# Loads moved: batch 2's k and v from batch 0's FFN to the start of batch 1's, and later loads a step or two back

## The chip, the cores and the metric

The kernel runs on one core of a Trainium2 chip. Its time is the device time of one execution in microseconds (us). An engine of the core takes its instructions strictly in the order of its own queue; the engines are TensorE (PE, with weight loads shown as PEld), VectorE (DVE), ScalarE (ACT), GpSimd (POOL) and SyncE (SP, which here issues nearly all DMAs). An instruction waits at the head of its queue until the semaphores it needs have arrived.

## The reference, cut to what matters

Attention with a packed query p (32 rows per head) in two softmax steps, then an FFN with softplus, for 8 batches of 576 tokens, 8 heads of 64, and a hidden width of 2048:

```python
p_packed = sm_attn(p, k, v)                # 32 packed rows per head
out = sm_attn(q, p_packed, p_packed)
x = out.transpose(0, 2, 1, 3).reshape(B * S, H * D)
h = x @ w_in
g = np.maximum(h, 0.0) + np.log1p(np.exp(-np.abs(h)))
return g @ w_out
```

The activations are float32. The weights are float64 and are converted on the chip.

## The kernel before, in words

**Stages.** Attention of batch 0 runs first, alone but for the conversion of the first weights. Then a loop runs over 128 units, 16 to a batch (variable `u`; unit u is batch u // 16, and f = u % 16 is a block of 128 hidden columns). A unit does `gemm1` (12 matmuls of line 585), the softplus of its two halves, and `gemm2_tile` for the unit two before it (12 matmuls of line 623). Every unit has four slots (the loop over t). In each slot a counter `due` grows by PACE = 0.56, and each time it passes 1 the attention of the next batch goes one step further: `attention_first` for batches 0 and 1, `attention_next` from batch 2 on (FIRST = 2). A step ends at a `yield`. So the attention of batch 1 runs inside the FFN of batch 0 (units 0 to 15), and that of batch 2 inside the FFN of batch 1 (units 16 to 31). What of it is left in the last unit of a batch is run to its end there, and `weights` then makes the operands of the next batch's gemm1.

**Weights.** In batch 0's FFN a second counter does the same with `convert`, 1.6 steps a slot. It goes through 32 blocks, named i0 to i15 for w_in and o0 to o15 for w_out, in the order i0 i1 o0 o1 i2 i3 o2 o3 and so on. A block is loaded into an x slot (`load64`, line 150, two DMAs for w_in, one for w_out); there are two such slots, so a block can only be loaded when the block two before it has been read. Then ACT makes m and r of it (lines 192, 196), DVE t (198, 203), POOL the sum (211), and for w_out ACT and DVE make the two halves (230, 236). `make_m` (line 548) reads the converted w_in: it runs on PE every second unit in batch 0, and the call at the end of unit 10 needs i12 and i13, the one at the end of unit 12 needs i14 and i15.

**Loads.** q, k and v have one pool of four buffers, `ld`. Each tile is half a batch (four heads). A load takes the buffer of the tile that was used up last: batch 2's two k tiles take those of batch 1's v, which are free after `packed` (line 310), and batch 2's two v tiles those of batch 1's q. From batch 2 on, k and q come as four DMAs of 144 KB each (line 137) and are turned by DVE in place (`quads`, line 246), and v as one DMA of 576 KB (line 129). Before the change, k of the next batch is loaded in the step that runs `packed`, v in the step before `scores2` (batch 1's attention) or with it (later), and q right behind the two `scores1` that read k. `load_pack` loads p for two batches with two DMAs (line 99), in the last unit of every second batch.

**Order.** PE's order is that of the text of the program: the kernel is built under `manual_schedule` for PE alone. For the other queues, DVE, ACT, POOL and SP with its DMAs, a planner lays down a fixed order when the kernel is built: it plays the program through with its own estimates of time, gives every engine what is ready, and among ready instructions the one that stands first in the text. On the chip that order does not change any more.

Where batch 2's loads stand in the text before: k half 0 in unit 5, k half 1 in unit 8, v half 0 in unit 9, v half 1 in unit 12. Among them stand the loads of the blocks o10 to o15 and i12 to i15.

Of the kernel before, what the change touches and what calls it, by code (L numbers as in the profile page):

```python
# [26 lines left out]
def pack_attention_then_softplus_ffn(  # L27
# [19 lines left out]
    G = H * J // P  # L47
# [7 lines left out]
    FIRST = 2  # L55
# [186 lines left out]
    def quads(nm, b, g):  # L242
        t = loaded[nm, b, g]
        for o in range(0, HG, 2):
            x = t[:, o:o + 2, :].rearrange("x h n -> x (h n)")
            nc.vector.transpose(x, x)
        return [t[:, hh, :] for hh in range(HG)]
# [113 lines left out]
    def attention_first(b):  # L361


        a1 = [work.tile([P, S], F32, tag="a1", name=f"a1_{b}_{g}") for g in range(G)]
        pp = [None] * G
        kT, qT = [], []
        for hh in range(HG):
            kT.append(transposed("k", b, 0, hh))
            yield
        load("q", b, 0)  # L370
        for c in range(2):
            scores1(b, 0, c, kT, a1[0])
        yield
        nm = softmax1_max(b, 0, a1[0])
        kT = [transposed("k", b, 1, 0)]
        yield
        z0 = softmax1_exp(b, 0, a1[0], nm)
        kT.append(transposed("k", b, 1, 1))
        yield
        rs0 = softmax1_sum(b, 0, z0)  # L380
        for hh in range(2, HG):
            kT.append(transposed("k", b, 1, hh))
            yield
        load("q", b, 1)
        for c in range(2):
            scores1(b, 1, c, kT, a1[1])
        yield
        nm = softmax1_max(b, 1, a1[1])
        a1T = work.tile([NP, SI, P], F32, tag="a1T", name=f"a1T_{b}_0", bufs=1)
        for c in range(2):  # L390
            a1_transposed(b, 0, c, a1[0], a1T)
            yield
            if c == 0:
                z1 = softmax1_exp(b, 1, a1[1], nm)
        rs1 = softmax1_sum(b, 1, z1)
        pp[0] = packed(b, 0, a1T, rs0)
        load("k", b + 1, 0)
        yield
        qT.append(transposed("q", b, 0, 0))
        yield  # L400
        a1T = work.tile([NP, SI, P], F32, tag="a1T", name=f"a1T_{b}_1", bufs=1)
        for c in range(2):
            a1_transposed(b, 1, c, a1[1], a1T)
            yield
        res[b]["pt"].append(packed_transposed(b, 0, pp[0]))
        yield
        qT.append(transposed("q", b, 0, 1))
        yield
        pp[1] = packed(b, 1, a1T, rs1)
        load("k", b + 1, 1)  # L410
        yield
        for hh in range(2, HG):
            qT.append(transposed("q", b, 0, hh))
            yield
        load("v", b + 1, 0)
        a2 = scores2(b, 0, 0, qT)
        a2n = scores2(b, 0, 1, qT)
        yield
        softmax2_exp(b, 0, 0, a2)
        res[b]["pt"].append(packed_transposed(b, 1, pp[1]))  # L420
        yield
        qT = [transposed("q", b, 1, 0)]
        softmax2_div(b, 0, 0, a2)
        a2 = a2n
        yield
        qT.append(transposed("q", b, 1, 1))
        softmax2_exp(b, 0, 1, a2)
        yield
        qT.append(transposed("q", b, 1, 2))
        yield  # L430
        qT.append(transposed("q", b, 1, 3))
        softmax2_div(b, 0, 1, a2)
        yield
        load("v", b + 1, 1)
        a2 = scores2(b, 1, 0, qT)
        a2n = scores2(b, 1, 1, qT)
        yield
        softmax2_exp(b, 1, 0, a2)
        yield
        softmax2_exp(b, 1, 1, a2n)  # L440
        softmax2_div(b, 1, 0, a2)
        yield
        softmax2_div(b, 1, 1, a2n)
        yield

    def attention_next(b):


        a1 = [work.tile([P, S], F32, tag="a1", name=f"a1_{b}_{g}") for g in range(G)]
        kT = [quads("k", b, 0)]  # L450
        yield
        yield
        for c in range(2):
            scores1(b, 0, c, kT[0], a1[0])
        load("q", b, 0)
        yield
        nm = softmax1_max(b, 0, a1[0])
        kT.append(quads("k", b, 1))
        yield
        z0 = softmax1_exp(b, 0, a1[0], nm)  # L460
        yield
        for c in range(2):
            scores1(b, 1, c, kT[1], a1[1])
        load("q", b, 1)
        yield
        rs0 = softmax1_sum(b, 0, z0)
        nm = softmax1_max(b, 1, a1[1])
        yield
        a1T = work.tile([NP, SI, P], F32, tag="a1T", name=f"a1T_{b}_0", bufs=1)
        for c in range(2):  # L470
            a1_transposed(b, 0, c, a1[0], a1T)
            yield
            if c == 0:
                z1 = softmax1_exp(b, 1, a1[1], nm)
        yield
        rs1 = softmax1_sum(b, 1, z1)
        pp = [packed(b, 0, a1T, rs0)]
        load("k", b + 1, 0)
        qT = [quads("q", b, 0)]
        yield  # L480
        a1T = work.tile([NP, SI, P], F32, tag="a1T", name=f"a1T_{b}_1", bufs=1)
        for c in range(2):
            a1_transposed(b, 1, c, a1[1], a1T)
            yield
        res[b]["pt"].append(packed_transposed(b, 0, pp[0]))
        yield
        pp.append(packed(b, 1, a1T, rs1))
        load("k", b + 1, 1)
        qT.append(quads("q", b, 1))
        yield  # L490
        a2 = scores2(b, 0, 0, qT[0])
        a2n = scores2(b, 0, 1, qT[0])
        load("v", b + 1, 0)
        yield
        res[b]["pt"].append(packed_transposed(b, 1, pp[1]))
        yield
        softmax2_exp(b, 0, 0, a2)
        yield
        softmax2_div(b, 0, 0, a2)
        yield  # L500
        softmax2_exp(b, 0, 1, a2n)
        yield
        softmax2_div(b, 0, 1, a2n)
        yield
        a2 = scores2(b, 1, 0, qT[1])
        a2n = scores2(b, 1, 1, qT[1])
        load("v", b + 1, 1)
        yield
        softmax2_exp(b, 1, 0, a2)
        yield  # L510
        softmax2_div(b, 1, 0, a2)
        yield
        softmax2_exp(b, 1, 1, a2n)
        yield
        softmax2_div(b, 1, 1, a2n)
        yield
# [154 lines left out]
    for f in range(NF):  # L671
        if f % 2 == 0:
            order += [("i", f), ("i", f + 1)]
        order.append(("o", f))
    PACE = 0.56
    CONV = 1.6
    CONV_EARLY = 1.6
    CONV_STEP = 14
# [14 lines left out]
    due = 0.0  # L693
# [12 lines left out]
    ahead, chain, due = iter(()), iter(()), 0.0  # L706
    for u in range(len(units) + LAG):
        if u < len(units):
            b, f = units[u]
            if f == 0:  # L710
                if (b + 1) % BG == 0 and b + 1 < B:
                    pack_transposed((b + 1) // BG, pt)
                ahead = attention(b + 1) if b + 1 < B else iter(())
                due = 0.0
            chain = softplus(b, f, gemm1(b, f, res[b]), gs)
            next(chain)
            if f == NF - 1:
                if (b + 2) % BG == 0 and b + 2 < B:
                    pt = load_pack((b + 2) // BG, (nc.sync,))
                for _ in ahead:  # L720
                    pass
                if b + 1 < B:
                    weights(b + 1)
        if u >= LAG:
            b2, f2 = units[u - LAG]
            gh, gl = gs.pop((b2, f2))
            if f2 == 0:
                acc = [ps_acc.tile([P, DM], F32, tag="acc", name=f"acc_{b2}_{t}") for t in range(NT)]
        last = u >= LAG and f2 == NF - 1 and b2 % 2 == 1
        if last:  # L730
            both = rests(b2)
            next(both)
        for t in range(NT):
            if u >= LAG:
                gemm2_tile(
                    acc[t], gh, gl, f2, slice(t * P, (t + 1) * P), f2 == 0, f2 == NF - 1
                )
                if f2 == NF - 1:
                    store(acc[t], [(0, b2, t * P, P)], f"{b2}_{t}")
            if u < len(units):  # L740
                due += PACE
                while due >= 1:
                    next(ahead, None)
                    due -= 1
                if b == 0:
                    cdue += CONV
                    while cdue >= 1:
                        next(conv, None)
                        cdue -= 1
            next(chain, None)  # L750
        if last:
            next(both)
        if u + 2 < len(units):


            nb, c = units[u + 2][0], units[u + 2][1] * P
            if c % m_cols(nb) == 0:
                make_m(nb, c // m_cols(nb), res[nb])
# [29 lines left out]
```

## Time and profile before

| | |
|---|---|
| time, median of 3 runs | 816.55 us (815.74 to 820.81) |
| profiled execution | 816.35 us, span 814.6 us, mean granted clock 0.963 |
| PE busy | 743.3 us, 91% |
| DVE busy | 540.4 us, 66% |
| ACT busy | 440.6 us, 54% |
| POOL busy | 93.8 us, 12% |
| HBM read, written | 45.61 MB, 9.44 MB |

The page divides the span into 40 slices and gives each engine's busy share in tenths; 9 means 90% or more. The other views used below are: sums over stretches of the span; the waits, which give for each instruction that waited the one that released it, with the total in us, the count and the longest; and the timeline, with start and duration in us, engine, line of the kernel, operation and tiles, and in square brackets the idle time before it with its releaser. A tile is written by its name in the program: m, r and t are the steps of the conversion, x_i and x_o are raw weight blocks, psm is make_m's product, ps that of the scores, T_q a transposed q, a the attention scores.

The starts of units given below are those of the first matmul of line 585 of a unit.

### The profile page before, as it was taken

How to read it: one execution, taken by the hardware profiler on the slowest of the kernel's cores; microseconds unless marked ns; L12 is line 12 of the kernel's file. 1: busy time of each engine (PE TensorE's matmuls, PEld its weight loads, DVE VectorE, ACT ScalarE, POOL GpSimd, SP SyncE). 2: the span in 40 equal slices, each digit the busy share in tenths (PEclk: the TensorE clock that was granted, in tenths of full speed). 3: DMA queues.
4: the chain of work that ended last, by engine and by line, in shares of the span. 5: the costliest groups of instructions: out<-in, count | busy, mean ns of one | idle time of the engine just before them, and what ended most of it. 6: DMA issues, size and time to landing. Idle time of an engine off the chain costs nothing.

```text
span 814.6 us, 14337 instructions
## 1 busy us (share of the span) xinstructions
PE 743.3 (91%) x5360; PEld 585.6 (72%) x5360; DVE 540.4 (66%) x1220; ACT 440.6 (54%) x1089; POOL 93.8 (12%) x166
## 2 busy tenths in 40 slices
PE   5478994499999989999999999999999899999997
PEld 3256674277788767886788777877788687887886
DVE  3688866856696647856686647766786647665544
ACT  6558854566555345565555345565556254565550
POOL 1414321310000000000000000100000000001010
PEclk9968996699999989999999999999999999999999
DMA  9976834505410334105410333105410310010002
GB/s 230 237 164 158 191 88 101 133 14 111 89 30 1 82 52 79 30 8 111 89 30 2 83 64 64 31 17 103 80 30 1 89 35 2 1 39 14 1 1 65
DMA packets 149669, 55.97 MB, mean 69 GB/s; under 512 B 116320, under 2 KB 142944, under 8 KB 149600
## 3 DMA queue, kind: packets, MB, share of 16 engines
q1 hardware_dynamic: 149328, 55.00, 30.5%
q8 instruction: 42, 0.69, 0.4%
q14 instruction: 27, 0.22, 0.1%
q10 hardware_dynamic: 272, 0.07, 0.0%
HBM read 45.61 MB, written 9.44 MB: 68 GB/s over the span
## 4 chain that ended last, share of the span: by engine, by line
PE 81%; DVE 9%; ACT 4%; DMA 3%; issue 2%; POOL 1%; SPq 0%; DVEq 0%; ACTq 0%; POOLq 0%
PE acc L623 40%; PE ph L585 26%; PE acc_m L623 5%; PE psm L548 4%; PE ps L267 2%; DMA x_o<-in_moe_w_out 2%; PE psp L310 1%; DVE t L203 1%; DVE wo_l L236 1%; DMA x_i<-in_moe_w_in 1%; PE psa L300 1%; ACT m L192 1%; DVE t L198 1%; POOL t L211 1%; DVE a L343 1%
## 5 line engine op out<-in xcount | busy, mean ns | idle before, releaser
L623 PE MATMUL acc<-wo_h,gh 128*128 128x512 f32 x512 | 208.9, 408 | 13.9 <-DVE nm L282 6.7
L612 DVE SCALAR_TENSOR_TENSOR e<-ph,e 128x288 f32<-128x288 f32 x256 | 113.6, 451 | 161.7 <-ACT e L610 160.8
L607 ACT ACTIVATE e<-ph 128x288 f32<-128x288 f32 x256 | 102.9, 403 | 186.2 <-PE ph L585 133.5
L623 PE MATMUL acc<-wo_l,gh 128*128 128x512 f32 x512 | 202.0, 395 | 0.0
L623 PE MATMUL acc<-wo_h,gl 128*128 128x512 f32 x512 | 201.5, 394 | 0.0
L585 PE MATMUL ph<-at_h,mh 128*128 128x288 f32 x512 | 160.8, 314 | 4.0 <-DVE e L612 2.7
L585 PE MATMUL ph<-at_l,mh 128*128 128x288 f32 x512 | 155.0, 303 | 4.6 <-DVE at_l L531 4.6
L585 PE MATMUL ph<-at_h,ml 128*128 128x288 f32 x512 | 154.7, 302 | 0.0
L585 PEld LDWEIGHTS ph<-at_h,mh 128*128 128x128 f32 x512 | 99.2, 194 | 42.8 <-issue 16.9
L623 PEld LDWEIGHTS acc<-wo_h,gh 128*128 128x128 f32 x512 | 97.1, 190 | 40.8 <-issue 7.9
L616 POOL COPY rest<-e 128x64 f32<-128x64 f32 x128 | 49.9, 390 | 611.0 <-DVE e L612 585.4
L623 PEld LDWEIGHTS acc<-wo_h,gl 128*128 128x128 f32 x512 | 96.8, 189 | 21.5
L609 ACT ACTIVATE e<-e 128x288 f32<-128x288 f32 (+1 forms) x240 | 109.1, 455 | 3.9
L610 ACT ACTIVATE e<-e 128x288 f32<-128x288 f32 (+1 forms) x240 | 109.2, 456 | 3.1
L623 PEld LDWEIGHTS acc<-wo_l,gh 128*128 128x128 f32 x512 | 97.3, 190 | 13.1
L585 PEld LDWEIGHTS ph<-at_l,mh 128*128 128x128 f32 x512 | 99.8, 195 | 7.8 <-DVE at_l L531 5.1
L585 PEld LDWEIGHTS ph<-at_h,ml 128*128 128x128 f32 x512 | 99.7, 195 | 0.0
L600 DVE TENSOR_TENSOR gl<-e,gh 128x512 fp32r<-128x512 f32 x128 | 91.3, 714 | 6.3
L563 ACT CAST mh<-psm 128x512 fp32r<-128x512 f32 (+1 forms) x72 | 35.7, 541 | 66.6 <-PE psm L548 66.6
L564 DVE TENSOR_TENSOR ml<-psm,mh 128x512 fp32r<-128x512 f32 (+1 forms) x72 | 42.6, 624 | 33.0 <-ACT mh L563 32.5
L548 PE MATMUL psm<-w_in_sb,pt 64*32 64x512 f32 (+1 forms) x576 | 42.8, 612 | 20.4 <-POOL w_in_sb L211 19.4
L599 DVE CAST gh<-e 128x512 fp32r<-128x512 f32 x128 | 55.1, 430 | 6.7 <-PE acc L623 0.5
(75 smaller groups left out, 720.5 us busy)
## 6 DMA issues: line engine op xcount, KB each, us to landing
v<-in_v SPq DMA_DIRECT2D x16, 576.0 KB, 4.7
x_i<-in_moe_w_in SPq DMA_DIRECT2D x32, 256.0 KB, 4.3
x_o<-in_moe_w_out SPq DMA_DIRECT2D x16, 512.0 KB, 4.6
k<-in_k SPq DMA_DIRECT2D x48, 144.0 KB, 3.1
q<-in_q SPq DMA_DIRECT2D x48, 144.0 KB, 3.2
out<-o SPq DMA_DIRECT2D x18, 256.0 KB, 2.2
k<-in_k SPq DMA_DIRECT2D x4, 576.0 KB, 9.8
q<-in_q SPq DMA_DIRECT2D x4, 576.0 KB, 8.8
```

What stands on the lines that cost most here:

```text
L548: nc.tensor.matmul(ps[hh * J:(hh + 1) * J, :n], res["pt"][g][o:o + D, hh * J:(hh + 1) * J], w_in_sb[o:o + D, hh, c * n:(c + 1) * n], start ...
L563: nc.scalar.copy(mh[:, cols], ps[:, :n])
L564: nc.vector.tensor_tensor(ml[:, cols], ps[:, :n], mh[:, cols].bitcast(F32), op=ALU.subtract)
L585: nc.tensor.matmul(ph[:, :C], x[:, ms], y[:, g, cs], start=(i == 0), stop=(i == 3 * G - 1),)
L599: nc.vector.tensor_copy(hi, x)
L600: nc.vector.tensor_tensor(lo, x, hi.bitcast(F32), op=ALU.subtract)
L607: nc.scalar.activation(es[c], hv[c], AF.Abs)
L609: nc.scalar.activation(x, x, AF.Exp, scale=-1.0)
L610: nc.scalar.activation(x, x, AF.Ln, bias=1.0)
L612: nc.vector.scalar_tensor_tensor(es[c], hv[c], 0.0, es[c], op0=ALU.max, op1=ALU.add)
L616: nc.gpsimd.tensor_copy(rest[:, rest_at(b, f), r:r + REST], e[:, NT * P:])
L623: nc.tensor.matmul(acc, x[:, cs], y[:, f, :], start=(first and i == 0), stop=(last and i == 2),)
```

## The change

Four things are edited.

1. In `attention_first`, the loads of the next batch's k and v are only made if that batch is below FIRST. That leaves those for batch 1 and takes out those for batch 2.
2. In `attention_next`, batch 2 begins with its own loads, k half 0, k half 1, v half 0, v half 1, one to a step, and an empty step. In the text these are units 16 and 17 now. Everything else of batch 2's attention follows five steps later.
3. For batch 2's attention alone, the pace is 0.62 steps a slot (PACE_FIRST).
4. In `attention_next`, the loads stand further back. q half 0 and q half 1 move from the end of the step with `scores1` to the beginning of a step two on, k half 0 from the step with `packed` to the one after the second `a1_transposed`, k half 1 and v half 0 two steps back, v half 1 two steps back. No step is added or taken away by this.

```diff
@@ attention_first
-        load("k", b + 1, 0)
+        if b + 1 < FIRST:
+            load("k", b + 1, 0)
...
-        load("k", b + 1, 1)
+        if b + 1 < FIRST:
+            load("k", b + 1, 1)
...
-        load("v", b + 1, 0)
+        if b + 1 < FIRST:
+            load("v", b + 1, 0)
...
-        load("v", b + 1, 1)
+        if b + 1 < FIRST:
+            load("v", b + 1, 1)
@@ attention_next
+        if b == FIRST:
+            for nm in ("k", "v"):
+                for g in range(G):
+                    load(nm, b, g)
+                    yield
+            yield
         kT = [quads("k", b, 0)]
         yield
         yield
         for c in range(2):
             scores1(b, 0, c, kT[0], a1[0])
-        load("q", b, 0)
         yield
         nm = softmax1_max(b, 0, a1[0])
         kT.append(quads("k", b, 1))
         yield
+        load("q", b, 0)
         z0 = softmax1_exp(b, 0, a1[0], nm)
         yield
         for c in range(2):
             scores1(b, 1, c, kT[1], a1[1])
-        load("q", b, 1)
         yield
         rs0 = softmax1_sum(b, 0, z0)
         nm = softmax1_max(b, 1, a1[1])
         yield
+        load("q", b, 1)
...
         pp = [packed(b, 0, a1T, rs0)]
-        load("k", b + 1, 0)
         qT = [quads("q", b, 0)]
         yield
...
             a1_transposed(b, 1, c, a1[1], a1T)
             yield
+        load("k", b + 1, 0)
         res[b]["pt"].append(packed_transposed(b, 0, pp[0]))
         yield
         pp.append(packed(b, 1, a1T, rs1))
-        load("k", b + 1, 1)
         qT.append(quads("q", b, 1))
         yield
         a2 = scores2(b, 0, 0, qT[0])
         a2n = scores2(b, 0, 1, qT[0])
-        load("v", b + 1, 0)
         yield
+        load("k", b + 1, 1)
         res[b]["pt"].append(packed_transposed(b, 1, pp[1]))
         yield
+        load("v", b + 1, 0)
         softmax2_exp(b, 0, 0, a2)
...
         a2 = scores2(b, 1, 0, qT[1])
         a2n = scores2(b, 1, 1, qT[1])
-        load("v", b + 1, 1)
         yield
         softmax2_exp(b, 1, 0, a2)
         yield
+        load("v", b + 1, 1)
         softmax2_div(b, 1, 0, a2)
@@ the main loop
+    PACE_FIRST = 0.62
...
-                due += PACE
+                due += PACE if b != FIRST - 1 else PACE_FIRST
```

## The prediction, made before the change was run

> **What bounds the kernel now.** I read the page first: its 40 slices say where PE is not full.
>
> ```profile
> span 814.6 us, 14337 instructions
> PE   5478994499999989999999999999999899999997
> ```
>
> PE is the engine to keep busy, and from the ninth slice on it is (slices of 20.4 us). Before that it has two holes: slices one to three, which are the start of the kernel, and slices seven and eight, 122 to 163 us, near the end of batch 0's FFN. Next come sums over stretches, cut where a unit's gemm1 begins (unit 8 at 103.4, 10 at 116.0, 11 at 133.7, 12 at 140.2, 13 at 159.9, 16 at 177.9; then batches 1 and 3):
>
> ```profile
> 103.40:116.00 12.60, 12.60 (x139) 9.38 (x137) 6.55 (x16) 7.45 (x16) 0.97 (x3) 1.00 0.12 28
> 116.00:133.70 17.70, 6.03 (x52) 4.29 (x44) 15.41 (x33) 7.45 (x15) 5.70 (x5) 0.71 0.59 150
> 133.70:140.20 6.50, 6.50 (x38) 5.88 (x31) 1.87 (x5) 3.43 (x8) 0.19 (x1) 0.75 0.36 73
> 140.20:159.90 19.70, 8.85 (x60) 5.16 (x58) 17.17 (x36) 10.44 (x19) 5.71 (x6) 0.77 0.53 137
> 159.90:177.90 18.00, 17.24 (x104) 13.77 (x96) 10.02 (x21) 11.44 (x24) 3.49 (x4) 0.88 0.03 7
> 177.90:259.40 81.50, 81.50 (x625) 64.90 (x624) 59.03 (x136) 47.86 (x126) 5.64 (x17) 1.00 0.30 59
> 359.00:442.10 83.10, 81.50 (x624) 64.88 (x624) 58.62 (x135) 48.38 (x126) 6.35 (x16) 1.00 0.29 58
> ```
>
> The columns are the stretch, its length, then busy us of PE, PEld, DVE, ACT, POOL, then clock, DMA share, GB/s. Batch 1's FFN is PE from end to end (81.50 of 81.50); batch 3 leaves 1.6. Units 10 and 12 leave 11.7 and 10.85, with DVE at 87% in both. So what the change can win lies in two units of batch 0's FFN. The waits and the timeline say what ends them:
>
> ```profile
> PE psm L548 <- POOL w_in_sb L211: 19.4, 2, 11.7
> ...
> 147.37 1.20 PE L267 MATMUL ps<-T_q,pt 64*32 64x288 f32 x10 [3.11 <-ACT T_q L260]
> 158.87 1.11 PE L548 MATMUL psm<-w_in_sb,pt 64*32 64x256 f32 x16 [7.74 <-POOL w_in_sb L211]
> ```
>
> make_m waits 11.7 us in unit 10 and 7.7 in unit 12 for the last columns of w_in to be converted, and 3.1 for a transposed q that stands behind a conversion on ACT. So: why is the conversion late?
>
> ```profile
> 66.47 0.68 ACT L192 ACTIVATE m<-x_i 128x512 f32<-128x512 f32 x1
> ...
> 95.76 0.67 ACT L192 ACTIVATE m<-x_i 128x512 f32<-128x512 f32 x1
> ...
> 114.45 0.67 ACT L192 ACTIVATE m<-x_o 128x512 f32<-128x512 f32 x1
> ...
> 123.34 0.67 ACT L192 ACTIVATE m<-x_i 128x512 f32<-128x512 f32 x1
> ...
> 128.96 0.44 ACT L346 ACTIVATE a<-a 128x288 f32<-128x288 f32 x1 [4.40 <-DVE a L343]
> ```
>
> These are the first conversions of pairs of blocks (two x slots, so two blocks are in flight). From 66.47 to 95.76 four pairs pass, 7.3 us each. The next one takes 18.7, so 11.4 is lost exactly there. SP's own timeline shows what stands at that place:
>
> ```profile
> 90.54 3.35 SPq L150 DMA_DIRECT2D x_i<-in_moe_w_in  x4
> 93.93 4.01 SPq L137 DMA_DIRECT2D k<-in_k  x4
> 98.48 2.04 SPq L150 DMA_DIRECT2D x_o<-in_moe_w_out  x2
> 107.70 0.33 SPq L137 DMA_DIRECT2D k<-in_k  x1
> 115.71 4.06 SPq L150 DMA_DIRECT2D x_i<-in_moe_w_in  x4
> 119.82 3.12 SPq L137 DMA_DIRECT2D k<-in_k  x3
> 124.58 6.30 SPq L150 DMA_DIRECT2D x_o<-in_moe_w_out  x2
> 130.93 0.43 SPq L129 DMA_DIRECT2D v<-in_v  x1
> ...
> 164.08 14.75 SPq L99 DMA_DIRECT2D p<-in_p  x4
> 185.58 2.52 SPq L644 DMA_DIRECT2D out<-o  x4
> ```
>
> Batch 2's first k, four DMAs, goes ahead of the weights o10 and o11. But it does not delay them by much on the chip (the first two lines are of this window, the last is the page's median over all x_o):
>
> ```profile
> L150 SPq DMA_DIRECT2D x_o<-in_moe_w_out x2: 346/386/426, 98.5 to 100.2; - x2
> ...
> DMA to landing us min/median/max: 4.6/5.1/5.5
> ...
> x_o<-in_moe_w_out SPq DMA_DIRECT2D x16, 512.0 KB, 4.6
> ```
>
> o10 lands by 104.0 (98.5 + 5.5) and is touched at 114.45. ACT did not wait for it: its fixed order has this conversion behind the softplus of two more units. So the loss is the planner's. It expected the block late, behind four k pieces, and wrote ACT's order for that. 11.4 / 4 = 2.9 us a piece is my estimate of what it charged.
>
> [...]
>
> **What the change does to the queues.** In the program text batch 2's eight k DMAs and two v DMAs leave batch 0's FFN (units 5, 8, 9, 12) and stand at units 16 and 17. But only PE's order is the text's. The p row above has four DMAs, two calls of load_pack; the second is written in batch 2's last unit (47), and it stands ahead of the output stores of unit 17, at the moment its buffer is free. Batch 2's k is transposed in unit 9, though that is written in unit 16:
>
> ```profile
> 111.42 0.77 DVE L246 STREAM_TRANSPOSE k<-k 128x576 f32<-128x576 f32 x1
> ```
>
> So the other queues take what is ready, the earliest in the text first. Batch 2's k finds its buffer free after packed (L310) in unit 5, as now, and SP is idle then. It will not wait for unit 16. What changes is its rank: now the four pieces outrank o10; after, every weight load outranks every piece. The second k shows what a lower rank does: one piece (107.70), then four weight DMAs, then three pieces, and the pair behind it came at 123.34 - 114.45 = 8.9 us, only 1.6 over 7.3.
>
> **The sum**, against the profiled execution: 816.35 us with a span of 814.6, so 1.75 lies around it; it is 0.2 under the median of 816.55.
>
> - k2 and v2 out of rank. Bounds: nothing (all four pieces still slip in before o10 is ready), and all of both stalls. The upper one is limited by DVE: from 103.4 to 177.9 it has 6.55 + 15.41 + 1.87 + 17.17 + 10.02 = 51.0 us of work in 74.5; at the 87% it reaches in the stalls that is 58.6, a gain of 15.9, and 23.5 at 100%. I take the pattern of the second k: one piece ahead of the pair o10/o11 and one more ahead of i12/i13, 5.8 instead of 11.4, so i12 and i13 come 5.6 earlier and the wait of unit 10 falls from 11.7 to 6. For unit 12 (7.7 + 3.1) I take the same 5.6, since i14/i15 are the next pair but one on the same chain. Together 11.2. DVE then has 51.0 in 63.3, 81%, which it has shown it can do.
> - SP. The ten DMAs cost 4.01 + 0.33 + 3.12 on SP for k and 0.43 each for v, 8.3 us, wherever they stand. Should they really go to unit 16, they would stand behind p and ahead of the stores of 185.58, in a queue that is idle from 178.8; cost nothing there.
> - Batch 2's attention on PE. This order is the text's, so the five added steps do shift it: scores1 from unit 17 to unit 19, the last softmax step from unit 27 to 28, at 0.62 steps a slot instead of 0.56. weights(2) needs it in unit 31, ten slots later. PE's work is the same; what hides the shift is a batch that is PE alone (81.50 of 81.50). Without that cover I would give it batch 3's 1.6. I take 0, and keep 0 to 1.6.
> - q, k and v of batches 3 to 7, one or two steps later in the text: 18 DMAs a batch with a lower rank against the stores, and no other effect while SP takes what is ready. Bounds from the rows of PE's waits after 178 us: a loss of 1.6 a batch if a buffer comes late (k and v of a batch are loaded a whole FFN ahead of their use, q a few units ahead); a gain of what the stores cost now:
>
> ```profile
> PE acc L623 <- DVE o L640: 3.1, 2, 1.6
> ```
>
> I take 0, nearest to what readiness gives, and keep -3.1 to +1.6.
>
> 816.35 - 11.2 = 805.
>
> **The rivals.**
>
> Nothing moves (816, between 811 and 820). The planner issues four pieces in a row as soon as packed is done; o10's slot is free only when the conversion begun at 95.76 is over, and SP's four pieces ran from 93.93 to 97.94. For it: that near tie, and k x4 in one run. Against: the second k was split after one piece. This is also the case that the change does not do what it says.
>
> Clean (793 to 800). The weights never meet a piece, both stalls go, DVE bounds: 816.35 - 15.9 to 23.5. For it: the text's order, if it held. Against: p and k above are taken long before their place.
> The clock adds here: the 6.5 us of unit 11 ran full at 0.75 and the 17.24 after it at 0.88, 1.6 + 2.1 us that short stalls would give back.
> [...]
>
> Slower (828). The new order puts the conversion of i13 and of i15 behind a softmax step on ACT that itself waits on DVE, as i13 stands now behind the 4.40 us wait of 128.96. If one more such wait with its step (4.4 + 1.5) hits each of the two pairs, 2 x 5.9 = 12 us are lost. It decides when that exceeds the 5.6 a pair gains. Against: the wait came from conversions crowding DVE (87%), and earlier ones crowd it less.
>
> **How the numbers follow.** Partial gain (800 to 811) 0.42; nothing moves 0.35; clean, below 800, 0.12; slower, above 820, 0.11. The predicted time is the first case's, 805; its own range is 800 to 811. The range for 8 in 10 is 793 to 820: some 0.05 lies below, 0.11 above. A measurement can tell about 1% from no change, 808.4 to 824.7 here. Faster by more: 0.12 and four fifths of 0.42, 0.46. Slower by more: most of 0.11, 0.09. Within: 0.45.
>
> **What would show it.** Right: on SP the weights o10 and o11 stand behind fewer than four k pieces; ACT's conversion after 95.76 comes before 108; the two waits of psm for w_in_sb sum to 6 to 14 instead of 19.4; k of batch 2 is still loaded in batch 0's FFN; batch 1's FFN stays at 81.5 to 83. Wrong: SP has k x4 ahead of o10 again and the waits stand at 19 (nothing moves); no k before 164 us (the text's order holds, clean); or new waits of PE in batch 1's FFN, which I priced at nothing.

## The result, and the profile after

The changed kernel takes 784.58 us, median of 4 runs (781.94 to 786.86), against 816.14 us for the kernel before on the same chip: a ratio of 0.960, with an interval of 0.955 to 0.965. The forecast was 805 us with a range of 793 to 820; the direction was right, the gain is nearly three times the predicted one (31.6 us instead of 11.2), and the time lies below the range. One execution of one of the later kernels (the shift at the old pace), of 917.62 us at a granted clock of 0.765, is left out of all that follows.

The head of the page of the changed kernel, with the slices of PE and of its clock:

```profile
span 780.2 us, 14340 instructions
PE   6568998889999999999999999999999999999997
PEclk9999999999999999999999999999999999999999
```

The hole in slices seven and eight is gone, and no slice has a mean clock under 0.9. The span is cut at the same places in both traces, at the first gemm1 matmul of units 0 and 10 and of each batch (us, worked out from the traces):

| | start | units 0-9 | units 10-15 | batch 1 | 2 | 3 | 4 | 5 | 6 | 7 |
|---|---|---|---|---|---|---|---|---|---|---|
| before | 45.5 | 70.5 | 61.9 | 81.5 | 99.6 | 83.1 | 97.9 | 83.0 | 97.2 | 94.4 |
| after | 43.2 | 71.3 | 40.1 | 86.8 | 92.9 | 83.0 | 92.9 | 83.4 | 92.2 | 94.4 |
| difference | -2.3 | +0.8 | -21.8 | +5.3 | -6.7 | -0.1 | -5.0 | +0.4 | -5.0 | 0.0 |

The differences sum to the difference of the spans, 814.6 to 780.2. Three things happened: 21.8 us won in the last six units of batch 0's FFN, 16.7 won in the even batches 2, 4 and 6, and 5.3 lost in batch 1. The start ran from 43.2 to 46.3 us over all the kernels of this study, whose text is the same there, so its 2.3 is not put down to the change; nor are the 0.8 of units 0 to 9 and the 0.4 of batch 5, which ran from 83.0 to 85.9 over these kernels.

**Batch 0's FFN.** Sums over stretches of the changed kernel (columns as in the prediction's table of stretches; units 10 to 15, batch 1, batch 2), and below them the two stretches of the kernel before that the prediction did not show (units 10 to 15, batch 2):

```profile
114.50:154.70 40.20, 35.56 (x238) 26.38 (x230) 37.35 (x87) 27.70 (x59) 11.41 (x14) 0.96 0.54 129
154.70:241.40 86.70, 83.62 (x623) 65.32 (x623) 60.48 (x138) 48.00 (x126) 4.80 (x17) 1.00 0.28 56
241.40:334.30 92.90, 92.90 (x679) 74.05 (x678) 65.26 (x154) 47.65 (x125) 5.41 (x17) 1.00 0.27 54
```

```profile
116.00:177.90 61.90, 38.62 (x237) 29.09 (x229) 44.47 (x94) 32.76 (x66) 15.09 (x15) 0.78 0.38 96
259.40:359.00 99.60, 95.53 (x680) 75.50 (x678) 65.53 (x154) 48.16 (x125) 5.80 (x17) 0.97 0.25 50
```

In units 10 to 15 the granted clock rises from 0.78 to 0.96, and DVE is busy for 37.35 of 40.20: 93%. PE's idle time in these units falls from 23.3 us to 4.6 and its busy time from 38.62 to 35.56. SP's timeline of the changed kernel shows where the ten loads went:

```profile
88.18 3.37 SPq L150 DMA_DIRECT2D x_i<-in_moe_w_in  x4
91.59 0.60 SPq L137 DMA_DIRECT2D k<-in_k  x1
94.66 3.48 SPq L150 DMA_DIRECT2D x_o<-in_moe_w_out  x2
98.19 0.42 SPq L137 DMA_DIRECT2D k<-in_k  x1
...
141.98 0.81 SPq L99 DMA_DIRECT2D p<-in_p  x2
142.83 1.18 SPq L137 DMA_DIRECT2D k<-in_k  x2
144.10 1.58 SPq L129 DMA_DIRECT2D v<-in_v  x2
```

Batch 2's k is still loaded in batch 0's FFN, not at the start of batch 1's, but four of its eight pieces go one at a time between the weights, and the other four and v follow behind them. ACT's timeline, for i11 and i13 (the second of a pair of w_in; make_m at the end of unit 10 waits for i13), before and then after, where the row between them is the first conversion of o10:

```profile
98.90 0.67 ACT L192 ACTIVATE m<-x_i 128x512 f32<-128x512 f32 x1
...
129.31 0.64 ACT L192 ACTIVATE m<-x_i 128x512 f32<-128x512 f32 x1
```

```profile
96.54 0.68 ACT L192 ACTIVATE m<-x_i 128x512 f32<-128x512 f32 x1
100.01 0.66 ACT L192 ACTIVATE m<-x_o 128x512 f32<-128x512 f32 x1
...
113.79 0.71 ACT L192 ACTIVATE m<-x_i 128x512 f32<-128x512 f32 x1
```

From i11 to i13 it was 30.4 us and is 17.3; o10, touched at 114.45 before, is touched at 100.01. The waits of PE in this stretch name make_m's w_in once more, with 0.5 us instead of 19.4:

```profile
PE psm L558 <- POOL w_in_sb L211: 0.5, 1, 0.5
```

**The even batches.** Their FFN has the rests of two batches in it (tile acc_m), and its output o_m. SP's timeline in batch 2, before and after:

```profile
266.92 2.44 SPq L644 DMA_DIRECT2D out<-o  x4
269.44 2.99 SPq L137 DMA_DIRECT2D q<-in_q  x4
272.53 2.23 SPq L644 DMA_DIRECT2D out<-o  x4
...
288.30 1.11 SPq L644 DMA_DIRECT2D out<-o_m  x2
```

```profile
248.97 2.44 SPq L654 DMA_DIRECT2D out<-o  x4
251.50 0.54 SPq L137 DMA_DIRECT2D q<-in_q  x1
252.84 2.53 SPq L654 DMA_DIRECT2D out<-o  x4
...
262.77 1.11 SPq L654 DMA_DIRECT2D out<-o_m  x2
```

Before, the four DMAs of q half 0 stood ahead of the second half of the stores. On the timelines of PE and DVE the copy of o_m came late with it, before (first two fences) and after (third):

```profile
279.57 0.39 PE L623 MATMUL acc_m<-wo_h,gl_m 128*128 128x512 f32 x1
...
288.33 0.79 PE L623 MATMUL acc<-wo_h,gh 128*128 128x512 f32 x1 [4.07 <-DVE o_m L640]
...
289.91 1.96 PE L548 MATMUL psm<-w_in_sb,pt 64*32 64x512 f32 x16
```

```profile
282.47 0.46 DVE L612 SCALAR_TENSOR_TENSOR e<-ph,e 128x288 f32<-128x288 f32 x1 [4.59 <-ACT e L610]
...
285.99 1.44 DVE L246 STREAM_TRANSPOSE q<-q 128x576 f32<-128x576 f32 x2
...
287.58 0.69 DVE L640 COPY o_m<-acc_m 128x512 f32<-128x512 f32 x1
```

```profile
262.05 0.69 DVE L650 COPY o_m<-acc_m 128x512 f32<-128x512 f32 x1 [2.12 <-PE acc_m L633]
...
267.13 1.09 PE L558 MATMUL psm<-w_in_sb,pt 64*32 64x512 f32 x16
```

Before, the last matmul on acc_m ended at 280, and DVE stood idle for the 4.59 us up to 282.47: its fixed order had the copy behind a softplus and q's transposes. PE waited 4.07 us for it, and the next make_m ran for 1.96 us instead of the 1.09 of the kernel after; the clock was 0.50 for 5.7 us behind the wait (288.33 to 294.02). After, the copy waits for acc_m alone, and PE is busy for 92.90 of 92.90 us. Batches 4 and 6 lose time at the same place: before, DVE has q's transposes ahead of o_m's copy there too, and PE waits 3.37 and 3.38 us.

### The profile page after: what moved, and what is told of

Same layout as the page of the kernel before. It is cut to its first block, busy times and chain, and to the rows that moved or that the text cites. A ratio compares the mean times of both kernels' runs of the same rounds, so it can differ in the third digit from the quotient of the medians.

```text
span 780.2 us, 14340 instructions
## 1 busy us (share of the span) xinstructions
PE 737.2 (94%) x5360; PEld 580.6 (74%) x5360; DVE 536.8 (69%) x1220; ACT 437.0 (56%) x1089; POOL 93.9 (12%) x166
## 4 chain that ended last, share of the span: by engine, by line
PE 81%; DVE 8%; ACT 5%; DMA 3%; issue 2%; POOL 1%; SPq 0%; DVEq 0%; ACTq 0%; POOLq 0%
PE acc L633 40%; PE ph L595 25%; PE acc_m L633 6%; PE psm L558 4%; PE ps L267 2%; PE psp L310 1%; DMA q<-in_q 1%; PE psa L300 1%; DMA x_i<-in_moe_w_in 1%; DVE t L203 1%; ACT e L619 1%; DVE e L622 1%; ACT e L620 1%; ACT m L192 1%; DVE wo_l L236 1%
## 5 line engine op out<-in xcount | busy, mean ns | idle before, releaser
L595 PE MATMUL ph<-at_h,mh 128*128 128x288 f32 x512 | 158.7, 310 | 6.9 <-DVE e L622 5.5
L595 PE MATMUL ph<-at_l,mh 128*128 128x288 f32 x512 | 153.0, 299 | 4.3 <-DVE at_l L541 4.3
L595 PE MATMUL ph<-at_h,ml 128*128 128x288 f32 x512 | 153.1, 299 | 0.0
L595 PEld LDWEIGHTS ph<-at_h,mh 128*128 128x128 f32 x512 | 97.4, 190 | 42.9 <-issue 13.9
L626 POOL COPY rest<-e 128x64 f32<-128x64 f32 x128 | 48.3, 378 | 582.8 <-DVE e L622 551.4
L595 PEld LDWEIGHTS ph<-at_l,mh 128*128 128x128 f32 x512 | 97.8, 191 | 7.7 <-DVE at_l L541 5.0
L595 PEld LDWEIGHTS ph<-at_h,ml 128*128 128x128 f32 x512 | 97.8, 191 | 0.0
```

Of the source, the lines that this page charges most:

```text
L595: nc.tensor.matmul(ph[:, :C], x[:, ms], y[:, g, cs], start=(i == 0), stop=(i == 3 * G - 1),)
L626: nc.gpsimd.tensor_copy(rest[:, rest_at(b, f), r:r + REST], e[:, NT * P:])
```

## The experiments

The two theories are these. **Rank**: what counts is only which of the ready loads stands first in the text; the gains come from k and v standing behind the weights (batch 0) and q behind the stores (even batches), and the shift of batch 2's attention by five steps is a cost. **Place or shift** (the rival): the gain needs the loads out of batch 0's FFN, or the later attention. In the list, the stretches are those of the table above, and each ratio is to runs of the kernel before on the same chip, whose medians lay between 815.8 and 817.2 us.

**Rank alone.** Before, with the four loads taken out of `attention_first` and put at the head of batch 2's attention without a step of their own:

```diff
@@ attention_first
-        load("k", b + 1, 0)
+        if b + 1 < FIRST:
+            load("k", b + 1, 0)
...
@@ attention_next
+        if b == FIRST:
+            for nm in ("k", "v"):
+                for g in range(G):
+                    load(nm, b, g)
         kT = [quads("k", b, 0)]
```

> Batch 2's k and v loads stand in the text behind all weight loads (first step of batch 2's attention, no step added, pace 0.56, other loads as before). Theory 1 (the gain of batch 0's FFN is the lower rank of ten DMAs, not their place nor the later start): units 10 to 15 take about 40 us as in the changed kernel (61.9 before), batch 1 stays near 81.5, batches 2, 4 and 6 stay at 99.6, 97.9 and 97.2; time about 816.4 - 21.7 - 2.3 = 792. Rival (the gain needs the five empty steps or the slower rank of the later loads too): units 10 to 15 stay over 50 us and the time is over 804.

Measured: 794.46 us, ratio 0.972 (0.968 to 0.976). Units 10 to 15 took 38.8 us, batch 1 82.0, batches 2, 4 and 6 99.8, 96.3 and 98.4. So the rank alone gives all of batch 0's gain and none of the even batches', and costs 0.5 us in batch 1.

**Rank and steps.** The same with the five yields and the pace of the change:

```diff
                 for g in range(G):
                     load(nm, b, g)
+                    yield
+            yield
...
-                due += PACE
+                due += PACE if b != FIRST - 1 else PACE_FIRST
```

> The moved loads with the five steps and the pace of 0.62, later loads as before. Theory 1 (batch 1's extra 5.2 us comes from the shifted steps): batch 1 takes 86 to 87 us, batches 2, 4 and 6 as before; time about 5 over the kernel with the rank alone, 797. Rival (it comes from the later q loads): batch 1 at 81.5 to 82.5, time 792.

Measured: 803.41 us, ratio 0.983 (0.980 to 0.987). Units 10 to 15 stay at 38.7; batch 1 goes to 89.5. The steps add no gain and cost 7.5 us in batch 1, more than the 5 expected. What made the further 2.5 is not shown: PE's waits there are those of the changed kernel's batch 1 (2.5 us in two, 0.6 in one).

**Rank and later loads.** The changed kernel without the five steps and their pace:

```diff
                 for g in range(G):
                     load(nm, b, g)
-                    yield
-            yield
...
-                due += PACE if b != FIRST - 1 else PACE_FIRST
+                due += PACE
```

> The changed kernel without the five steps and with the pace of 0.56 throughout, so PE's order is that of the kernel before. Theory 1 (the shift of the steps costs, the other two parts gain): batch 1 near 81.5, batches 2, 4 and 6 at 92 to 93, time about 782 - 5 = 777, faster than both. Rival (batch 1's loss comes with the later q loads): batch 1 at 86, time 782 to 785.

Measured: 779.61 us, ratio 0.954 (0.950 to 0.957): less than the changed kernel's time. Units 10 to 15 at 38.7, batch 1 at 82.0, batches 2, 4 and 6 at 92.9, 92.9 and 92.2.

**Later loads alone.** Before, with only edit 4 of the change; batch 2's k and v where they were. The first and the last of the six moved lines:

```diff
             scores1(b, 0, c, kT[0], a1[0])
-        load("q", b, 0)
         yield
         nm = softmax1_max(b, 0, a1[0])
         kT.append(quads("k", b, 1))
         yield
+        load("q", b, 0)
...
-        load("v", b + 1, 1)
         yield
         softmax2_exp(b, 1, 0, a2)
         yield
+        load("v", b + 1, 1)
```

> Only the later loads of q, k, v in batches 3 to 7; batch 2's loads where they were. Theory 1 (parts add up): batch 0's FFN with both waits as before (units 10 to 15 about 62 us), batches 2, 4 and 6 at 92 to 93; time about 816.4 - 16.7 = 800. Rival (batches 2, 4 and 6 gain because batch 0 ran differently): they stay at 97 to 99 and the time is 816.

Measured: 798.32 us, ratio 0.977 (0.973 to 0.981). Units 10 to 15 took 64.4, with make_m waiting 19.8 us in two waits, the longer one 11.6, batch 1 81.5, and the even batches 92.9, 92.9 and 92.2. Stage by stage the two gains do not touch each other.

**Loads really held back.** Rank and later loads, with batch 2's ten loads made to follow the p loads of unit 15 in the order that is written down, so that they leave the weights' stretch in fact (`last_p` keeps the last DMA of `load_pack`):

```diff
         if b == FIRST:
-            for nm in ("k", "v"):
-                for g in range(G):
-                    load(nm, b, g)
+            with tc.issue_after(last_p[0].ins):
+                for nm in ("k", "v"):
+                    for g in range(G):
+                        load(nm, b, g)
```

> Rank and later loads, no added steps (779.6 us so far), and batch 2's ten loads held in SP's order behind the p loads, so that not one of them stands among the weight loads. Theory 1 (what cost was the planner's order for ACT and DVE behind four pieces in a row; one piece ahead of a pair of weights costs nothing that reaches PE, since DVE is over 90% busy there): units 10 to 15 take 37 to 40 us against 38.7, time 777 to 782. Rival (the pieces among the weights still cost as DMAs or delays): units 10 to 15 fall under 36, time under 776. Rival 2 (k then comes late): batch 1 takes over 84.

Measured: 787.18 us, ratio 0.965 (0.963 to 0.967). Units 10 to 15 take 38.3, less by 0.4 than with the pieces among the weights, or by 2.0 than in another profile of that kernel (40.3, side by side below); units 0 to 15 together take 110.7 against 110.1 and 110.2. So the low-ranked pieces cost next to nothing in this FFN. Batch 1 takes 88.8, and the time is above the 777 to 782 expected, as its second rival had it. Rows of SP's timeline, DVE's and PE's, and below them ACT's i11 and i13 with no piece among the weights:

```profile
141.56 6.86 SPq L139 DMA_DIRECT2D k<-in_k  x8
```

```profile
171.31 1.43 DVE L248 STREAM_TRANSPOSE k<-k 128x576 f32<-128x576 f32 x2
172.66 1.25 DVE L651 COPY o<-acc 128x512 f32<-128x512 f32 x2
...
173.37 0.79 PE L634 MATMUL acc<-wo_h,gh 128*128 128x512 f32 x1 [4.64 <-DVE o L651]
```

```profile
97.15 0.68 ACT L194 ACTIVATE m<-x_i 128x512 f32<-128x512 f32 x1
...
112.81 0.68 ACT L194 ACTIVATE m<-x_i 128x512 f32<-128x512 f32 x1
```

The later k puts its transposes ahead of two output copies on DVE, and PE waits 4.64 us for one of them. The loads are held here until 141.56, still before unit 16 (155.9), where the text of the change has them; held until there, they could only come later. As it is, nothing is won in batch 0's FFN and 6.8 us are lost in batch 1: the low rank without the place is better.

**First k high.** Rank and later loads, but k half 0's four DMAs back at their old place (unit 5), so that only they outrank the weights (`load` gets one more argument, the pieces to load):

```diff
             load("k", b + 1, 0)
+        else:
+            load("k", b + 1, 0, range(4))
...
         if b == FIRST:
-            for nm in ("k", "v"):
-                for g in range(G):
-                    load(nm, b, g)
+            load("k", b, 1)
+            for g in range(G):
+                load("v", b, g)
```

> As the kernel with rank and later loads, but half 0 of batch 2's k is back at its old place in the text, ahead of o10; half 1 and v stay behind all weights. Theory 1 (those four DMAs in a row are the cause): the first conversion after 93 to 96 us comes after 110 again, make_m's wait for w_in is 15 to 20 us, units 10 to 15 take 58 to 64. Rival (it takes the second k and v as well): units 10 to 15 under 50.

Measured: 787.48 us (two runs), ratio 0.965 (0.963 to 0.967). Units 10 to 15 took 50.4, less than expected. i11 and i13 on ACT, and make_m's waits:

```profile
98.18 0.68 ACT L194 ACTIVATE m<-x_i 128x512 f32<-128x512 f32 x1
...
128.59 0.64 ACT L194 ACTIVATE m<-x_i 128x512 f32<-128x512 f32 x1
```

```profile
PE psm L560 <- POOL w_in_sb L213: 13.5, 2, 11.6
```

From i11 to i13 it is the 30.4 us of before, and the first wait is there with 11.6. The second has 1.9 left of 7.7. So the first k makes the first stall by itself; most of the second stall needs the second k and v ranked high as well.

**Two pieces high.** The same with two of the four DMAs high and two low:

```diff
-            load("k", b + 1, 0, range(4))
+            load("k", b + 1, 0, range(2))
...
         if b == FIRST:
+            load("k", b, 0, range(2, P // Q))
             load("k", b, 1)
```

> The same with only two of the four DMAs of that half at the old place, the other two behind all weights. Linear price (2.9 us a piece, my estimate): the conversion behind them comes 3 to 6 us late and units 10 to 15 take about halfway between 38.7 and 62, so 48 to 52. Threshold (a slip is free until it uses up the lead of the conversions, some 4 us): 39 to 43.

Measured: 783.20 us (two runs), ratio 0.959 (0.957 to 0.962). Units 10 to 15 took 44.3, between the two expectations:

```profile
97.31 0.68 ACT L194 ACTIVATE m<-x_i 128x512 f32<-128x512 f32 x1
...
119.65 0.67 ACT L194 ACTIVATE m<-x_i 128x512 f32<-128x512 f32 x1
```

```profile
PE psm L561 <- POOL w_in_sb L213: 5.6, 2, 3.0
```

With no piece ahead of o10 (held back), one (the changed kernel), two and four, i13 comes 15.7, 17.3, 22.3 and 30.4 us after i11, and the first stall is 0, 0, 3.0 and 11.6 us. (In the three kernels with pieces, one more stands between o11 and i12.) Against no piece that is a delay of 1.6, 6.6 and 14.7: the first piece is cheap, the others take 4 to 5 us each, and of a delay the first 3 or so are covered (6.6 - 3.0, 14.7 - 11.6).

**Shift at the old pace.** The changed kernel with one number altered:

```diff
-    PACE_FIRST = 0.62
+    PACE_FIRST = 0.56
```

> The changed kernel with its five added steps, but a pace of 0.56 in batch 1 too. If the later start of batch 2's attention costs: batch 1 at 86 to 87 as in the changed kernel, 782 to 785 us. If the faster pace costs (more steps of attention in the units with the stores): batch 1 at 82 to 83 and 779 to 781 us.

Measured: 784.11 us, ratio 0.961 (0.958 to 0.964), batch 1 86.1. The cost of batch 1 is the shift's, not the pace's.

**q half 0 alone.** Rank alone, with one more line moved, the load of q half 0 from the step with `scores1` to the head of a step two on:

```diff
             scores1(b, 0, c, kT[0], a1[0])
-        load("q", b, 0)
         yield
         nm = softmax1_max(b, 0, a1[0])
         kT.append(quads("k", b, 1))
         yield
+        load("q", b, 0)
         z0 = softmax1_exp(b, 0, a1[0], nm)
```

> The kernel with the rank alone (794.5 us), and of all the later loads only half 0 of q, two steps back. Theory (the even batches gain because q's four DMAs no longer outrank the stores, so that acc_m is copied out before q is transposed on DVE): batches 2, 4 and 6 fall to 92 to 93 and the time to 777 to 781. Rival (k and v standing later matter as well): they stay over 95 and the time is over 786.

Measured: 778.13 us, ratio 0.954 (0.951 to 0.956). Batches 2, 4 and 6 at 92.9, 92.9 and 92.2, batch 1 at 82.0. This one line does all that edit 4 does; the other moved loads add nothing to it that can be measured.

**The changed kernel and the best version side by side.** The changed kernel once more, and rank with later loads once more, on one chip:

> The changed kernel itself, on one chip with the next one, for a direct comparison: 782 to 787 us, batch 1 at 86 to 87.

> Rank and later loads without the five steps, beside the changed kernel: 4 to 6 us less than it, 777 to 781 us, batch 1 at 82.

Measured: 784.20 us, ratio 0.961 (0.959 to 0.963), and 779.63, ratio 0.954 (0.953 to 0.956). The intervals do not meet: without the five steps the change is 4.6 us faster still. Batch 1 took 88.3 and 82.0. The 88.3 is over the 86 to 87 expected and over the changed kernel's first profile (86.8): PE's waits are the same (2.5 us in two, 0.6 in one), and the clock of the whole execution was 0.990 against 0.995; that the clock made the difference is not shown. The version with one moved q line (778.13) cannot be told from that.

## Why the prediction was right or wrong

**Where the time was, and why: right.** The stall of unit 10 hung on the four high-ranked k pieces ahead of o10, that of unit 12 mostly on the second k and v; the landing of o10 at 104.0, long before its first use, points to an order of ACT written for the pieces. Nothing was changed in the rank-alone kernel but the text's place of ten loads, and 22.7 us went (817.2 to 794.5). The step "what changes is its rank" was right too: the pieces are still taken in batch 0's FFN, and where they were truly held back, batch 0's FFN gained nothing more (110.7 us against 110.1 and 110.2).

**The first term of the sum, 11.2 us: the step that failed first.** It let one piece slip ahead of each of two pairs and left 5.8 us of the slip for that, at 2.9 a piece. One piece did slip in ahead of o10, as forecast, but i13 was then only 1.6 us later than with none. The number 2.9 was 11.4 divided by four, a straight line through one point; the prediction's own row of the second k had one piece at 1.6. And the sum took each us of slip for a us of stall, where some 3 are covered by the lead of the conversion over make_m. So both stalls went nearly whole: of 11.7 + 7.7 + 3.1 = 22.5, 0.5 us for w_in and 0.6 for a transposed q are left. That this is near the measured 21.8 (23.1 with the rank alone, 61.9 - 38.8) is partly luck: PE's idle time fell by only 18.6 us, since its waits for the softplus grew from 0.8 to 3.5, and 3.1 us came off its busy time, at a clock of 0.96 instead of 0.78. The second error in this term was its cap: it took the 87% that DVE reaches inside the stalls as the most that DVE can be filled. 87% was what the stalls allowed; with them gone it ran at 93% (37.35 of 40.20). The rival "clean" had the right size for this stage (15.9 to 23.5, measured 21.8) and the wrong reason: it wanted no piece between the weights.

**q, k and v of the later batches, taken as 0: the step that failed second, and its 16.7 us took the time out of the range.** The bound was drawn from one row of PE's waits after 178 us, that for the output copies, 3.1 us. Two more rows for acc stand beside it in the trace before the change:

```profile
PE acc L623 <- DVE nm L282: 6.7, 2, 3.4
PE acc L623 <- DVE o_m L640: 4.1, 1, 4.1
```

These are the waits behind o_m's copy, one in each even batch; in batches 4 and 6 the row names nm, which DVE makes right behind that copy (469.61 and 470.19 in batch 4). They sum to 10.8 us. The other 5.9 of the 16.7 went inside PE's busy time, and behind each of the three waits the clock was 0.50 for a time (from 287.2 to 294.0 in batch 2, from 471.5 to 474.9 in batch 4, from 652.4 to 655.8 in batch 6; 1.00 in the rest of these batches). The prediction's table has batches 1 and 3, which are free of it, and not batch 2. The line of sums for that batch, shown above, has 4.07 us without PE (99.60 less 95.53) and a clock of 0.97. With these rows the bound would have been over 10 us instead of 3.1. That one line on q is the whole of it is shown by the experiment; that the order of DVE put o_m's copy behind q because the stores, and with them o's two buffers, were expected later, is argued from the queue and not shown.

**Batch 2's five steps, taken as 0 to 1.6: wrong by more than its range.** Batch 1 takes 86.8 us (88.3 in a second profile) instead of 81.5, and the rank alone leaves it at 82.0. "A batch that is PE alone" was taken as cover. It was the opposite: with PE busy for 81.50 of 81.50 us the stage had no slack, and the waits that the new order made, 3.1 us, were paid in full. Waits of batch 1, and a place in unit 26 on PE's and DVE's timelines, after:

```profile
PE acc L633 <- DVE o L650: 2.5, 2, 1.4
PE psm L558 <- DVE a L334: 0.6, 1, 0.6
```

```profile
215.25 0.72 PE L267 MATMUL ps<-q,pt 64*32 64x288 f32 x16
216.54 1.94 PE L558 MATMUL psm<-w_in_sb,pt 64*32 64x512 f32 x16 [0.58 <-DVE a L334]
```

```profile
216.00 0.48 DVE L334 STREAM_TRANSPOSE a<-ps 128x288 f32<-128x288 f32 x1
...
216.89 0.47 DVE L334 STREAM_TRANSPOSE a<-ps 128x288 f32<-128x288 f32 x1
```

Of the 5.2 us between the two stretches (86.70 and 81.50), 3.1 are these waits. The other 2.1 are inside PE's busy time (83.62 against 81.50). Unit 26 shows how: the shift has put `scores2` right ahead of make_m. Both take their result tiles from one pool of two buffers (`bank`, line 92), so make_m waits 0.58 us for DVE to turn the first half of the scores out. The second half is out at 217.36, within the time of its sixteen matmuls, which take 1.94 us where 1.09 is usual: 0.85 more. The make_m at 193.36 takes 1.70 us, 0.61 more, right behind `a1_transposed`, which draws on the same pool, and the `scores2` at 203.97 takes 0.96 instead of 0.72. That the pool is the cause is read from the order of these rows, not tested; the remaining 0.4 us stay open. The prediction named new waits of PE in batch 1's FFN as what would make it wrong, and priced them at nothing.

**SP, taken as 0: right.** Held back, the ten DMAs took 8.4 us of SP (6.86 for k, 1.5 for v) with nothing waiting for the queue; what was late then was k itself.

**The other rivals.** Nothing moved is out by the rank-alone kernel, and slower for a conversion behind a DVE-bound step did not come up: make_m's wait is 0.5 us. The range ended at 793 because the first term was held near half and the even batches at zero. Put in as measured, the terms (-21.8, -16.7, +5.3, and -2.3 of scatter in the start) give 816.35 - 35.5 = 780.85, against the profiled 781.94; the scatter of units 0 to 9 and of batches 3 and 5, +1.1, is the rest.

## What to carry to other kernels

Where an order is written down beforehand, the place of a load in the text is a rank among loads that are ready, not a time: rank loads that are not urgent below those that an engine's fixed order hangs on (22.7 us here), and below the stores that free its buffers (16.3 us, 794.46 to 778.13). Landing time against first use (104.0 against 114.45) tells an order that expected the transfer late from a transfer that is late. And take the sums of every stage before a term is set to 0: 4 us without PE in batch 2 were in the trace before the change, and batch 1, in which PE was full, had nothing to hide a shift of its work (5.3 us).

## What the hardware showed that was not expected

In two of these traces a wait of 2 to 3 us was followed by half the clock. In the kernel with two pieces high, PE waits 3.04 us up to 124.07, and the clock is 0.50 from then to 130 (sums over stretches, columns as above):

```profile
124.00:130.00 6.00, 5.93 (x35) 4.73 (x36) 6.00 (x13) 3.15 (x8) 1.37 (x2) 0.50 0.34 87
```

In the changed kernel a wait of 2.01 us up to 142.42 is followed by the same, and later: the clock falls only between 143.5 and 144, some 1.4 us after the work has gone on, and is 0.50 for the next 3 us. PE's timeline, and a stretch:

```profile
142.42 0.40 PE L595 MATMUL ph<-at_h,mh 128*128 128x288 f32 x1 [2.01 <-DVE e L622]
```

```profile
144.00:147.00 3.00, 3.00 (x10) 2.43 (x9) 2.99 (x11) 2.36 (x5) 0.00 (x0) 0.50 0.92 163
```

But the same wait of 2.0 us, with rank alone and with rank and later loads, is followed by no fall: over units 10 to 15 the clock is 1.00 in both (116.90 to 155.70 and 114.90 to 153.60). Nor is any wait of the changed kernel after 147.24, of which the longest is 1.9 us: its clock is 1.00 from there to 778. What decides is not shown by these runs.

A short wait cost more here than the waits view says: in batch 4 of the kernel before, the wait of 3.37 us came with 1.6 us more inside PE's busy time (94.53 against 92.90 after), and the clock was 0.50 from 471.5 to 474.9.
